# A scratch tile of the weight conversion in PSUM, three banks for the first products, and memsets on GpSimd, in a gated attention and expert kernel

## The chip, the core and the metric

The kernel runs on one core of a Trainium2 chip. The metric is the device time of one execution in microseconds. TensorE multiplies matrices, VectorE and ScalarE work elementwise on SBUF and PSUM, GpSimd elementwise on SBUF, and SyncE (SP) issues nearly all DMAs. PSUM has eight banks of 512 fp32 values in each of 128 partitions.

## What is computed

Three stages follow each other (the reference, cut):

```python
for t in range(S):                                   # gated linear attention, S = 768, 32 heads of 48
    state = f[t][..., None] * state + outer(k[t], v[t])
    y[t] = q[t] @ state
x = y as (3072, 384)
e_idx = argmax(x @ w_gate)                           # one of 8 experts for each token
for e in range(8):
    h = maximum(x[e_idx == e] @ w1[e], 0)            # 384 -> 1024
    x[e_idx == e] = gate * eom * (h @ w2[e])         # 1024 -> 384
h = x @ w_in                                         # 384 -> 2048
out = (h * cos(h)) @ w_out                           # 2048 -> 384
```

All is fp32. The kernel gets fp32 precision from TensorE by splitting every operand into a rounded part (`hi`, `wh`, `yh`) and the rest (`lo`, `wl`, `yl`) and adding three products.

## The kernel before, in words

The attention stage ends near 182 us. It scatters its tokens into a DRAM table `xs` that is sorted by expert. Then comes the stage of the experts, in `moe_ffn`, until near 450 us, and after it the last feed-forward network (FFN).

The experts' stage has NS = 64 steps, 8 for each of 8 experts. A loop at the end of the stage runs, for each step s:

- `mm1(s)` (the first product): nine matmuls of 448 columns (L628, L629, L631, in the helper `first_product`) into a bank of the pool `ps_h`. ScalarE writes `hi` = relu (L190) and VectorE `lo` (L191); both read the bank, `lo` last. The pool has four banks.
- `mm2(s - 2)` (the second product): nine matmuls (L202 to L204) from `hi` and `lo` of step s - 2 into three banks `o`, which hold the expert's sum over its 8 steps. After an expert's last step VectorE and ScalarE copy the sums into `yT` (L212 to L215), at a place that is read from a register.
- the events listed for the step by `at(s, ...)`, called by one line, L326, in the order in which they were listed.

So the order on each engine's queue is written out by hand. The events are:

- Weights. A ring of split weights is filled some ten half blocks ahead. In each step a half block of 128 x 768 that lies in `ws` is split: ScalarE rounds two quarters (L114), GpSimd subtracts for the first, VectorE for the second (both L118). Then SP issues the next load into the `ws` buffer that comes free (L101), and waits for both subtractions before it.
- Tokens of the next expert. At step 8e + 7 SP writes a list of token numbers (L180) and issues four loads `xe` (L163). In steps 8e + 4 to 8e + 6 TensorE transposes 128 columns each (`trans_x`, L170) into the one bank of `ps_t`; ScalarE and VectorE split it (L620 and L621). The next transposition needs the bank empty.
- Conversion of the FFN's weights. They arrive in a 64-bit form, and 24 pieces of 128 x 512 are turned into fp32 and stored to DRAM. `conv_load` (L221) is three steps ahead of `conv_a`, and `conv_b` and `conv_store` (L246) follow a step after that; a piece starts every 2.3 steps from step 6 on. The two buffers of `cs` are freed by `conv_b`.
- In steps 0 to 5 twelve memsets clear `yT`, two in a step, after the step's split.

A conversion is one ScalarE instruction, Abs into the tile `a` (L228), and seven of VectorE: L229 writes the sign bits of `cs` into the tile `b`, L230 and L231 change `a` in place, L233 puts `a` and `b` together into `a`; then in `conv_b` L239 writes the exponents of `a` into `b`, L240 multiplies `b` with the low words of `cs`, L242 adds `b` to `a`. In the profile the tiles are called `ca` and `cb`. Both lie in SBUF; `cb` has one buffer.

PSUM is full in this stage: three banks `ps_o`, four `ps_h`, one `ps_t`.

Of the kernel before, what the change touches and what calls it, by code (L numbers as in the profile page):

```python
# [9 lines left out]
I32 = mybir.dt.int32  # L10
# [4 lines left out]
PSUM = bass.MemoryType.PSUM  # L15
# [32 lines left out]
def build(tc, A, O):  # L48
    nc = tc.nc
    sp = nc.sync  # L50
    with ExitStack() as top:
        const = top.enter_context(tc.tile_pool(name="const", bufs=1))
        dram = top.enter_context(tc.tile_pool(name="dram", bufs=1, space=DRAM))
        xs = dram.tile([XROWS, XW], F32, name="xs")
        idtab = dram.tile([NT + CAP, 1], I32, name="idtab")
        wffn = dram.tile([8, 128, PW], F32, name="wffn")

        ident = const.tile([128, 128], F32, name="ident")
        ones = const.tile([128, 128], BF16, name="ones")
        zeros = const.tile([128, 128], BF16, name="zeros")  # L60
        ctab = const.tile([128, E, GMAX], F32, name="ctab")
        acc = const.tile([128, E], BF16, name="acc")
        plast = const.tile([128, NU, NP], F32, name="plast")
        flag = const.tile([128, 1], I32, name="flag")

        with tc.manual_schedule(), ExitStack() as rows:
            c = dict(locals())
            c["W"] = W = Weights(tc, A, c, top)
            c["ya"] = top.enter_context(tc.tile_pool(name="ya", bufs=1, side="right"))
            c["xa"] = rows.enter_context(tc.tile_pool(name="xa", bufs=1, side="right"))  # L70
            attention(tc, A, c)
            W.more(top)
            moe_ffn(tc, A, O, c)
        general(tc, A, O, c)
# [50 lines left out]
def moe_ffn(tc, A, O, c):  # L125
    nc = tc.nc
    pe, dve, act, pool, sp = nc.tensor, nc.vector, nc.scalar, nc.gpsimd, nc.sync
# [4 lines left out]
    HP = PW // 3  # L132
    LAG1 = 2
    with ExitStack() as ctx:
        keep = ctx.enter_context(tc.tile_pool(name="keep", bufs=1))
        yT = keep.tile([128, KD, NT + CAP], F32, name="yT")
        start = keep.tile([128, E], I32, name="start")
        flag = c["flag"]
        reuse = dict(reuse_waits="tile")
# [10 lines left out]
        with ExitStack() as mctx:  # L150
            xb = mctx.enter_context(tc.tile_pool(name="xb", bufs=1, **reuse))
            cv = mctx.enter_context(tc.tile_pool(name="cv", bufs=1, **reuse))
            hp = mctx.enter_context(tc.tile_pool(name="hp", bufs=LAG1 + 1, **reuse))
            ps_o = mctx.enter_context(tc.tile_pool(name="ps_o", bufs=1, space=PSUM, **reuse))
            ps_h = mctx.enter_context(tc.tile_pool(name="ps_h", bufs=4, space=PSUM, **reuse))
            ps_t = mctx.enter_context(tc.tile_pool(name="ps_t", bufs=1, space=PSUM, **reuse))

            xe, xT, hh, yps = {}, {0: c["xT0"]}, {}, {}
# [65 lines left out]
            def conv_a(i):  # L224
                v = cvt[i].bitcast(I32).rearrange("p (n two) -> p n two", two=2)
                a = cv.tile([128, HP], F32, name="ca", bufs=2)
                b = cv.tile([128, HP], I32, name="cb")
                act.activation(out=a, in_=v[:, :, 1].bitcast(F32), func=AF.Abs)  # L228
                dve.tensor_scalar(out=b, in0=v[:, :, 1], scalar1=-2 ** 31, scalar2=None, op0=ALU.bitwise_and)  # L229
                dve.tensor_scalar(out=a, in0=a, scalar1=F64_LO, scalar2=F64_HI, op0=ALU.max, op1=ALU.min)  # L230
                dve.tensor_scalar(out=a.bitcast(I32), in0=a.bitcast(I32), scalar1=0x08000000, scalar2=3,  # L231
                                  op0=ALU.bitwise_xor, op1=ALU.logical_shift_left)
                dve.scalar_tensor_tensor(out=a.bitcast(I32), in0=a.bitcast(I32), scalar=0x7FFFFFFF, in1=b,  # L233
                                         op0=ALU.bitwise_and, op1=ALU.bitwise_or)
                cvt[i] = (v[:, :, 0], a, b)
# [43 lines left out]
            def at(s, fn, *a):  # L279
                ev.setdefault(s, []).append((fn, a))  # L280
# [7 lines left out]
            for i in range(24):  # L288
                t = 6 + 23 * i // 10
                at(t - 3, conv_load, i)  # L290
                at(t, conv_a, i)
                at(t + 1, conv_b, i)
                at(t + 1, conv_store, i)
# [13 lines left out]
            at(3, ids, 0)  # L307
            q = (NT + CAP) // 4
            for i in range(12):
                at(i // 2, dve.memset, yT[:, i // 4, i % 4 * q:(i % 4 + 1) * q], 0.0)  # L310
            for e in range(E - 1):
                for d in range(KD):
                    at(8 * e + 4 + d, trans_x, e + 1, d)
# [20 lines left out]
        with ExitStack() as fctx:  # L334
# [4 lines left out]
            ps_h = fctx.enter_context(tc.tile_pool(name="ps_h2", bufs=4, space=PSUM, **reuse))  # L339
# [871 lines left out]
```

## Time and profile before

| what | us |
| --- | --- |
| three runs | 848.99, 855.98, 854.69 |
| median | 854.69 |
| the profiled execution | 861.5 |
| its span | 859.3 |

The profiled execution's time is its span and 2.2 us around it. Over the span TensorE is busy for 823.4 us (96%), VectorE for 667.9 (78%), ScalarE for 380.6 (44%), GpSimd for 357.4 (42%). A busy TensorE says little by itself: its records overlap, and they are longer when the granted clock is lower, so the idle time and the clock are read together. [...] In a row of the timeline, what stands in brackets is the engine's idle time before the instruction and what ended it. In a row by line, three durations are the shortest, the median and the longest; a duration holds the time in which the instruction was held up on its engine.

### The profile page before, as it was taken

The numbers are of one execution on the slowest core, as the hardware profiler recorded it, in microseconds if no ns is written. First come the engines' busy times: TensorE is split into PE (matmuls) and PEld (weight loads), VectorE is DVE, ScalarE is ACT, GpSimd is POOL, SyncE is SP. The second block draws the span as 40 slices with busy tenths as digits, with TensorE's granted clock in tenths as the row PEclk, the third lists the DMA queues.
The fourth block names the chain that finished last, engine by engine and source line by source line (L and its number), as shares of the span: only waits on it lengthen the run. The fifth ranks groups of instructions, "written<-read, shape, count | busy, mean of one in ns | idle before, by whom it ended". The sixth has DMA issues, their size and how long they took to land.

```text
span 859.3 us, 14492 instructions
## 1 busy us (share of the span) xinstructions
PE 823.4 (96%) x5316; PEld 736.0 (86%) x5316; DVE 667.9 (78%) x1213; ACT 380.6 (44%) x737; POOL 357.4 (42%) x331
## 2 busy tenths in 40 slices
PE   7998999999889988989999999999999999999996
PEld 6886888878788988979998999999999999998886
DVE  5576787779778898789969887777787687788990
ACT  5574776464434434344544443333333333333440
POOL 5014443332213222232246665455455554455752
PEclk9998999999989999999999999999999999999999
DMA  8996775238787877769751000000000000000001
GB/s 197 342 314 173 201 190 151 75 112 176 175 160 245 180 186 232 133 211 218 182 137 38 2 0 28 10 1 19 19 1 19 19 1 11 28 1 9 29 1 42
DMA packets 45298, 91.69 MB, mean 107 GB/s; under 512 B 12864, under 2 KB 23232, under 8 KB 45216
## 3 DMA queue, kind: packets, MB, share of 16 engines
q1 hardware_dynamic: 42144, 81.20, 36.1%
q0 software_dynamic: 3072, 9.45, 3.0%
q8 instruction: 44, 0.72, 0.4%
q14 instruction: 38, 0.31, 0.1%
HBM read 69.34 MB, written 21.29 MB: 105 GB/s over the span
## 4 chain that ended last, share of the span: by engine, by line
PE 71%; DVE 12%; DMA 10%; issue 4%; ACT 2%; POOL 1%; SPq 0%; POOLq 0%; DVEq 0%; ACTq 0%
PE ps L628 9%; PE ps L629 9%; PE ps L631 9%; PE o L380 7%; PE o L378 7%; PE o L379 7%; DMA cs<-in_wffn 4%; PE xps L839 3%; PE sps L752 3%; PE o L202 2%; DMA ws<-in_wmoe 2%; PE o L203 2%; PE o L204 2%; PE yps L791 2%; PE yps L801 2%
## 5 line engine op out<-in xcount | busy, mean ns | idle before, releaser
L374 POOL TENSOR_TENSOR lo<-r,hi 128x512 fp32r<-128x512 f32 (+1 forms) x96 | 149.3, 1555 | 171.0 <-ACT hi L373 91.5
L118 POOL TENSOR_TENSOR wl<-ws,wh 128x384 fp32r<-128x384 f32 x96 | 102.7, 1070 | 220.2 <-ACT wh L114 173.1
L628 PE MATMUL ps<-yh,wh 128*128 128x512 f32 (+1 forms) x480 | 187.2, 390 | 0.3 <-ACT yh L620 0.3
L629 PE MATMUL ps<-yh,wl 128*128 128x512 f32 (+1 forms) x480 | 185.4, 386 | 0.0
L631 PE MATMUL ps<-yl,wh 128*128 128x512 f32 (+1 forms) x480 | 132.8, 385 | 0.0
L373 ACT CAST hi<-r 128x512 fp32r<-128x512 f32 (+1 forms) x96 | 56.2, 586 | 168.5 <-DVE r L368 166.6
L380 PE MATMUL o<-wh,lo 128*128 128x384 f32 x352 | 119.2, 339 | 0.9 <-POOL lo L374 0.5
L636 DVE TENSOR_SCALAR n<-ps 128x512 f32<-128x512 f32 x96 | 66.2, 690 | 68.6 <-PE ps L631 68.6
L378 PE MATMUL o<-wl,hi 128*128 128x384 f32 x352 | 118.6, 337 | 0.0
L379 PE MATMUL o<-wh,hi 128*128 128x384 f32 x352 | 118.4, 336 | 0.0
L631 PEld LDWEIGHTS ps<-yl,wh 128*128 128x128 f32 x480 | 91.3, 190 | 15.8
L644 ACT ACTIVATE r<-r,quarter 128x512 f32<-128x512 f32 x96 | 69.5, 724 | 73.5 <-DVE r L643 73.5
L628 PEld LDWEIGHTS ps<-yh,wh 128*128 128x128 f32 x480 | 91.5, 191 | 11.7 <-ACT yh L620 0.4
L629 PEld LDWEIGHTS ps<-yh,wl 128*128 128x128 f32 x480 | 91.4, 190 | 11.0
L114 ACT CAST wh<-ws 128x384 fp32r<-128x384 f32 x160 | 75.0, 510 | 0.4 <-DMA ws<-in_wmoe 0.4
L643 DVE SCALAR_TENSOR_TENSOR r<-n,r 128x512 f32<-128x512 f32 x96 | 69.5, 724 | 3.3
L190 ACT ACTIVATE hi<-ps 128x448 fp32r<-128x448 f32 x64 | 34.9, 545 | 82.8 <-PE ps L631 82.8
L204 PE MATMUL o<-lo,wh 128*128 128x448 f32 x192 | 70.4, 367 | 0.7 <-DVE lo L191 0.7
L202 PE MATMUL o<-hi,wh 128*128 128x448 f32 x192 | 70.9, 369 | 0.0
L203 PE MATMUL o<-hi,wl 128*128 128x448 f32 x192 | 70.7, 368 | 0.0
L379 PEld LDWEIGHTS o<-wh,hi 128*128 128x128 f32 x352 | 66.1, 188 | 4.3
L378 PEld LDWEIGHTS o<-wl,hi 128*128 128x128 f32 x352 | 66.2, 188 | 3.9
(159 smaller groups left out, 1451.2 us busy)
## 6 DMA issues: line engine op xcount, KB each, us to landing
ws<-in_wmoe SPq DMA_DIRECT2D x64, 384.0 KB
cs<-in_wffn SPq DMA_DIRECT2D x24, 512.0 KB
kq<-in_qkf SPq DMA_DIRECT2D x46, 192.0 KB
wffn<-ca SPq DMA_DIRECT2D x24, 256.0 KB
ws<-wffn SPq DMA_DIRECT2D x16, 384.0 KB
xs<-xe SPq DMA_DIRECT2D x7, 770.0 KB
v<-in_v SPq DMA_DIRECT2D x24, 200.0 KB
xe<-xs SPq DMA_DIRECT2D x28, 168.4 KB
```

Source lines behind the costliest of these rows:

```text
L114: self.nc.scalar.copy(out=h, in_=w)
L118: (eng or self.nc.gpsimd).tensor_tensor(out=l, in0=w, in1=h.bitcast(F32), op=ALU.subtract)
L202: pe.matmul(yps[e][d], wh[:, cs], hi, start=m == 0, stop=False)
L203: pe.matmul(yps[e][d], wl[:, cs], hi, start=False, stop=False)
L204: pe.matmul(yps[e][d], wh[:, cs], lo, start=False, stop=m == FT - 1)
L374: pool.tensor_tensor(out=los, in0=r[:, cs], in1=his.bitcast(F32), op=ALU.subtract)
L378: pe.matmul(o, hi, wl[:, cs], start=m == 0, stop=False)
L379: pe.matmul(o, hi, wh[:, cs], start=False, stop=False)
L380: pe.matmul(o, lo, wh[:, cs], start=False, stop=m == NF - 1)
L628: nc.tensor.matmul(out, wh[:, ws[d]], xh[:, d, :], start=d == 0, stop=False)
L629: nc.tensor.matmul(out, wl[:, ws[d]], xh[:, d, :], start=False, stop=False)
L631: nc.tensor.matmul(out, wh[:, ws[d]], xl[:, d, :], start=False, stop=d == 2)
```

## The change

The tile `b` of the conversion comes from a new PSUM pool of one bank, in place of SBUF. The pool of the first products has three banks in place of four. The twelve memsets of `yT` go from VectorE's queue to GpSimd's, at the same places in the order.

```diff
-            ps_h = mctx.enter_context(tc.tile_pool(name="ps_h", bufs=4, space=PSUM, **reuse))
+            ps_h = mctx.enter_context(tc.tile_pool(name="ps_h", bufs=3, space=PSUM, **reuse))
+            ps_c = mctx.enter_context(tc.tile_pool(name="ps_v", bufs=1, space=PSUM, **reuse))
...
                 a = cv.tile([128, HP], F32, name="ca", bufs=2)
-                b = cv.tile([128, HP], I32, name="cb")
+                b = ps_c.tile([128, HP], I32, name="cb")
...
             for i in range(12):
-                at(i // 2, dve.memset, yT[:, i // 4, i % 4 * q:(i % 4 + 1) * q], 0.0)
+                at(i // 2, pool.memset, yT[:, i // 4, i % 4 * q:(i % 4 + 1) * q], 0.0)
```

## Rows read from the trace of the kernel before

**Rows 1.** Stretches: stretch, length, busy PE, PEld, DVE, ACT, POOL, PEclk, DMA, GB/s

```profile
182.00:450.00 268.00, 251.92 (x1243) 229.78 (x1243) 227.75 (x357) 121.05 (x260) 78.72 (x77) 0.97 0.74 185
...
262.00:282.00 20.00, 18.42 (x98) 16.82 (x97) 18.25 (x29) 9.51 (x20) 6.15 (x6) 1.00 0.60 192
...
302.00:322.00 20.00, 17.78 (x85) 16.15 (x84) 18.49 (x33) 8.16 (x17) 4.95 (x5) 0.91 0.81 200
```

**Rows 2.** Waits of TensorE, 182 to 450 us: total us, times, longest

```profile
PE ps L170 <- DVE yl L621: 15.1, 6, 5.3
PE o L204 <- DVE lo L191: 0.7, 1, 0.7
PE ps L628 <- ACT yh L620: 0.3, 1, 0.3
```

**Rows 3.** TensorE's timeline, the six waits of a transposition: start, us

```profile
202.39 0.60 PE L170 MATMUL ps<-ident,xe 112*128 112x112 f32 x4 [0.91 <-DVE yl L621]
...
238.53 1.01 PE L170 MATMUL ps<-ident,xe 112*128 112x112 f32 x4 [5.33 <-DVE yl L621]
...
273.33 0.60 PE L170 MATMUL ps<-ident,xe 112*128 112x112 f32 x4 [1.58 <-DVE yl L621]
...
306.18 1.01 PE L170 MATMUL ps<-ident,xe 112*128 112x112 f32 x4 [2.22 <-DVE yl L621]
...
340.39 1.01 PE L170 MATMUL ps<-ident,xe 112*128 112x112 f32 x4 [2.28 <-DVE yl L621]
...
376.18 0.60 PE L170 MATMUL ps<-ident,xe 112*128 112x112 f32 x4 [2.79 <-DVE yl L621]
```

**Rows 4.** VectorE's timeline, from the run ahead of the second wait

```profile
226.43 0.43 DVE L229 TENSOR_SCALAR cb<-cs 128x512 int32<-128x512 int32 x1 [3.85 <-DMA cs<-in_wffn]
...
228.91 1.47 DVE L233 SCALAR_TENSOR_TENSOR ca<-ca,cb 128x512 int32<-128x512 int32 x1
...
233.18 1.43 DVE L242 TENSOR_TENSOR ca<-ca,cb 128x512 f32<-128x512 f32 x1
...
237.86 0.62 DVE L621 TENSOR_TENSOR yl<-ps,yh 128x448 fp32r<-128x448 f32 x1
```

**Rows 5.** By line, tile `cb`: shortest, median, longest ns

```profile
L229 DVE TENSOR_SCALAR cb<-cs x24: 408/418/428, 206.1 to 427.7; 128x512 int32<-128x512 int32 x24
...
L239 DVE TENSOR_SCALAR cb<-ca x24: 409/418/1198, 210.2 to 432.5; 128x512 int32<-128x512 int32 x24
...
L240 DVE SCALAR_TENSOR_TENSOR cb<-cs,cb x24: 691/693/1395, 211.2 to 433.0; 128x512 f32<-128x512 uint32 x24
```

**Rows 6.** Memsets by line (shortest, median, longest ns); one row of GpSimd's timeline

```profile
L326 DVE MEMSET yT<- x12: 792/792/792, 187.4 to 204.4; 128x880 f32 x12
...
L1012 POOL MEMSET xe<- x1: 1390/1390/1390, 10.4 to 10.4; 128x1540 f32 x1
...
193.01 1.01 POOL L118 TENSOR_TENSOR wl<-ws,wh 128x384 fp32r<-128x384 f32 x1 [2.64 <-ACT wh L114]
```

**Rows 7.** By line, VectorE in the FFN: shortest, median, longest ns

```profile
L636 DVE TENSOR_SCALAR n<-ps x96: 677/691/692, 451.5 to 833.2; 128x512 f32<-128x512 f32 x96
...
L368 DVE TENSOR_TENSOR r<-r,ps x96: 672/679/686, 455.1 to 837.6; 128x512 f32<-128x512 f32 x96
...
L637 DVE TENSOR_SCALAR n<-n x96: 426/427/1220, 452.2 to 833.9; 128x512 f32<-128x512 f32 x96
```

**Rows 8.** Groups of VectorE, 182 to 450 us: busy us, mean ns, idle before

```profile
L242 DVE TENSOR_TENSOR ca<-ca,cb 128x512 f32<-128x512 f32 x24 | 22.2, 925 | 0.8
...
L233 DVE SCALAR_TENSOR_TENSOR ca<-ca,cb 128x512 int32<-128x512 int32 x24 | 22.1, 919 | 0.8
...
L239 DVE TENSOR_SCALAR cb<-ca 128x512 int32<-128x512 int32 x24 | 17.3, 719 | 0.0
```

**Rows 9.** SP: a row of its waits, and one of its timeline

```profile
SPq L101 <- DVE wl L118: 116.0, 37, 13.3
...
213.34 0.35 SPq L221 DMA_DIRECT2D cs<-in_wffn  x1
```

## The prediction

> **What bounds the kernel now.** I read the stage table first, since the change touches the experts' stage alone. Between 182 and 450 us TensorE is busy for 251.9 of 268 us at a mean granted clock of 0.97 [rows 1]. The reader is to see two losses: 16.1 us of idle TensorE, and clock worth about 268 x 0.03 = 8.0 us. Without both the stage would take 244 us, so nothing done here can bring more than 24.1 us. Outside the stage the change touches nothing.
>
> Then the waits of TensorE [rows 2]: 15.1 us, in six waits, go to one pair: a transposition of the next expert's tokens (L170) waits until VectorE has emptied the only transposition bank (L621); 0.7 us more is one wait for `lo`. The timeline gives the six by size: 0.91, 5.33, 1.58, 2.22, 2.28 and 2.79 us [rows 3]. I call them A to F. Of the four larger ones the clock is the second price: the 20 us around D were granted 0.91, so 1.8 us more is lost there, those around C were granted 1.00 [rows 1]; an idle of 1.58 us cost no clock and one of 2.22 us did.
>
> Why L621 is late is in VectorE's timeline [rows 4]. Ahead of A VectorE is behind with memsets. Ahead of B it waits 3.85 us for a load of `cs` and then works back to back from 226.43 until L621 at 237.86, 11.4 us, while TensorE stands from 233.2 to 238.5 [rows 3]. In that run the two-input conversion steps L233 and L242 take 1.47 and 1.43 us, where such a step takes 0.69 undisturbed (L240's median) [rows 5]: GpSimd's split (L118) runs beside it. So the stage waits for a VectorE that is itself stretched by GpSimd. C to F have such a run ahead of them too.
>
> **The change part by part.**
>
> *Memsets.* Twelve of 0.792 us leave VectorE, 9.5 us, two in each of the steps 0 to 5 [rows 6]. A disappears: -0.9 us. On GpSimd a row of 1540 elements took 1.39 us [rows 6]; 880 elements are 0.79 by size alone, and I take 0.85, with 1.39 as the far end. Two in each step, 1.7 us, stand behind the step's split, in front of the next one's; from step 3 on GpSimd has 2.64 us idle there [rows 6], which hides even 2 x 1.39 but for 0.1 us. In steps 0 to 2 the splits come closer and two of them are pushed back by 1 to 2 us; who waits is SP's next `ws` load (L101), which today waits for VectorE's half of the split, itself behind the memsets. I take nothing for it. If that cover were gone, it is 2 us of load time once. The copies into yT (L212 to L215) now wait for GpSimd as well, but only after an expert's eighth step, when the memsets are over.
>
> *Three banks.* Nothing, and neither loss nor gain: before the first product of step s TensorE has already run the second product of step s-3, which needed that step's `lo`, and `lo` is the last reader of the bank that step s takes back. The wait is met by program order. The trace has no wait of a first product for its bank [rows 2].
>
> *The second tile in PSUM.* Five of the seven VectorE instructions of a conversion name it. Three (L233, L240, L242) had two inputs in SBUF and get one from PSUM. VectorE instructions with one input of each kind exist in the next stage: L368 stays between 672 and 686 ns in all 96 cases, while the SBUF-only L637 beside it is stretched from 426 to as much as 1220 [rows 7]. So the stretch should go: L233 from a mean of 919 to about 690, L242 from 925 to about 690 [rows 8]. The other two (L229, L239) lose: both run at 409 to 418 ns undisturbed from SBUF to SBUF [rows 5]; the only single-input row that touches PSUM, L636, takes 691 [rows 7]. No row shows VectorE writing to PSUM, so the price lies between 418 (no loss) and, far off, 1.395 us, the longest L240 [rows 5]. I take 690, the nearest row, for the three that write it. Over 24 conversions: +6.5 us (L229), 24 x (690 - 719) = -0.7 us (L239, whose mean is stretched today too), -5.5 us (L233), -5.6 us (L242) [rows 8]: -5.3 us of VectorE time in all, little for an engine that is busy 228 of 268 us. The 2-input and SBUF-only steps that remain (L118, L230, L231) are still open to GpSimd.
>
> What counts is the run ahead of each wait. Counted in the timeline there are ten stretched instructions of the freed kinds: L233, L240, L242 in B's run, two L233 in C's, one L233 in D's, L233 and L242 in each of E's and F's; each is some 0.75 us too long [rows 4]. Against them stand six L239 at +0.28 us (two ahead of C, one ahead of each of the others), and two L229 at +0.27 us, one each ahead of B and C; the other L229 start with a late load, and their extra is covered by ScalarE's Abs, for which L230 waits anyway. So:
> A 0.91 -> 0; B 5.33 - 2.25 + 0.55 = 3.6; C 1.58 - 1.5 + 0.83 = 0.9; D 2.22 - 0.75 + 0.28 = 1.75; E 2.28 - 1.5 + 0.28 = 1.05; F 2.79 - 1.5 + 0.28 = 1.55. The 0.7 us ahead of F (a wait for `lo`, behind L233) goes too.
> Idle falls from 15.8 to 8.85, by 7.0 us. D to F come down to the size of C, which cost no clock: three times 1.8 = 5.4 us of the 8.0 come back; 0 if the clock falls all the same. Sum: -12.4 us, or -7.0 if no clock comes back.
>
> [...]
>
> The profiled execution took 861.5 us, the runs' median is 854.69. If the difference is stage idle too, the runs lose 17.3 us where the profile loses 24.1, and the gain scales to 8.9 us: 845.8. Unscaled it is 842.3. I take **845.0 us**.
>
> **The rivals.**
> *Every wait goes (about 838 us).* SP waits 116 us for VectorE's splits before `ws` loads [rows 9], and the `cs` loads and the conversions' stores queue behind those; a VectorE that is earlier brings its own next load earlier. If that feeds on itself, all 24.1 us come back: 861.5 - 24.1 = 837.4. Against: B is set by a load that SP issued at 213.34 and that landed at 226.4 [rows 4, 9].
> *Loads set it (about 853 us).* B begins with VectorE idle for `cs` [rows 4]; D and F do as well. If the transfers, not the issue, are late, a faster VectorE waits longer and only A and a part of the runs go: 1 to 3 us. Against: after the landing VectorE works back to back, and its length is what TensorE waits for.
> *The conflict moves (about 860 us).* GpSimd's splits, one in each step, still need about 1 us each [rows 6] with the shared access. If they now meet L118, L230 and L231 instead, the ten stretches stay and the full-rate price comes on top: B +0.55, C +0.83, D to F +0.28 each, less A, +1.3 us; C comes to 2.4 us and loses 1.8 us of clock as D does; the stores and loads that come later for it repeat some 2 us: about +5. It decides once more than about half of the 7.5 us is paid elsewhere. A PSUM write of over 1.2 us would do the same: the runs hold fourteen uncovered ones (two L229, six L239, six L240), and 14 x 0.5 us eats the 7.0.
> *Not doing what it says*: if the PSUM input did not free VectorE from GpSimd, L233 and L242 would keep means over 0.9 us; that comes to the former case.
>
> **How the numbers follow.** Forecast (840 to 850) 0.45, every wait goes 0.13, loads set it 0.27, the conflict moves 0.15. Over 1%, about what a measurement of this kernel can tell from no change, means below 846.1 or above 863.2. Three quarters of the forecast's chance and all of the first rival lie below: 0.47. Of the last rival a half lies above: 0.07. The rest, 0.46, is within. The range reaches from 837 (all idle gone) to 859 (most of the moved conflict).
>
> **What would show it.** Right: L233, L240 and L242 within 20 ns of 680 to 695; L229 and L239 near 690; yT's memsets near 0.85 us on GpSimd; the wait at 202 us gone; L170's waits for L621 at some 9 us, and a clock of 0.98 or better in the stage. Wrong: L118 on VectorE well above its present mean, L621's waits at 15 us or more, a first product waiting for VectorE or ScalarE at its bank, or as much idle before L229 as saved elsewhere.

## The result, and the profile after

| what | before | after |
| --- | --- | --- |
| runs | 6 | 6 |
| median, us | 854.25 | 847.51 |
| lowest and highest, us | 848.99 and 856.55 | 843.90 and 849.42 |
| profiled execution, us | 861.5 | 847.61 |
| its experts' stage, us | 266.7 | 255.2 |

The ratio is 0.990, with a 95% interval of 0.9872 to 0.9928: 6 to 11 us faster. The profiled executions lie 13.9 us apart. Of that 11.6 us are the experts' stage, counted from its first product to the FFN's first product, and 2.7 us are the attention stage, which was just shorter in the second execution (the stage began at 179.82 in place of 182.50) and which the change doesn't touch. The profiled execution of the kernel before is also 5 us longer than the longest of its six runs. Such shifts between executions are why the medians and ratios decide below and the profiles only explain.

From the pools of PSUM on, lines of the kernel after are one higher than before: L229 to L242 of a conversion are L230 to L243, L170 is L171, L621 is L622, L326 is L327.

The whole stage first, from its own first product on; columns as in [rows 1]. Before, in a span of 859.3 us:

```profile
182.50:449.22 266.72, 250.95 (x1238) 229.04 (x1239) 227.33 (x355) 120.28 (x258) 78.43 (x75) 0.97 0.74 186
```

After:

```profile
179.82:434.97 255.15, 246.51 (x1237) 225.66 (x1238) 209.36 (x343) 120.67 (x258) 83.47 (x87) 0.99 0.77 194
```

Between these two executions TensorE's idle time falls from 15.8 to 8.6 us and its clock rises from 0.97 to 0.99. VectorE is busy 18.0 us less, GpSimd 5.0 us more. The waits of TensorE in the stage, which answer to [rows 2]:

```profile
PE ps L171 <- DVE yl L622: 8.6, 4, 4.1
PE ps L629 <- ACT yh L621: 0.3, 1, 0.3
```

In its timeline, the four that answer to the six of [rows 3]:

```profile
233.49 0.60 PE L171 MATMUL ps<-ident,xe 112*128 112x112 f32 x4 [4.14 <-DVE yl L622]
...
327.12 0.60 PE L171 MATMUL ps<-ident,xe 112*128 112x112 f32 x4 [0.33 <-DVE yl L622]
...
360.57 1.01 PE L171 MATMUL ps<-ident,xe 112*128 112x112 f32 x4 [2.81 <-DVE yl L622]
...
393.98 0.60 PE L171 MATMUL ps<-ident,xe 112*128 112x112 f32 x4 [1.36 <-DVE yl L622]
```

The first wait of before, near 202 us, is gone; the largest is 4.14 in place of 5.33. The steps that name `cb`, by line (shortest, median, longest ns), answer to [rows 5]:

```profile
L230 DVE TENSOR_SCALAR cb<-cs x24: 679/684/697, 202.1 to 414.0; 128x512 int32<-128x512 int32 x24
L234 DVE SCALAR_TENSOR_TENSOR ca<-ca,cb x24: 686/689/690, 204.3 to 416.5; 128x512 int32<-128x512 int32 x24
L240 DVE TENSOR_SCALAR cb<-ca x24: 676/683/685, 206.5 to 418.3; 128x512 int32<-128x512 int32 x24
L241 DVE SCALAR_TENSOR_TENSOR cb<-cs,cb x24: 695/696/697, 207.2 to 419.0; 128x512 f32<-128x512 uint32 x24
L243 DVE TENSOR_TENSOR ca<-ca,cb x24: 686/686/687, 207.9 to 419.7; 128x512 f32<-128x512 f32 x24
```

No step is stretched any more: the longest of the 120 takes 697 ns, where the longest of before took over 1.4 us. The two single-input steps went from 418 to 684 ns. The largest run of before [rows 4] has its counterpart in VectorE's timeline:

```profile
222.90 0.69 DVE L230 TENSOR_SCALAR cb<-cs 128x512 int32<-128x512 int32 x1 [4.56 <-DMA cs<-in_wffn]
...
225.38 0.69 DVE L234 SCALAR_TENSOR_TENSOR ca<-ca,cb 128x512 int32<-128x512 int32 x1
...
228.63 0.69 DVE L243 TENSOR_TENSOR ca<-ca,cb 128x512 f32<-128x512 f32 x1
...
232.82 0.62 DVE L622 TENSOR_TENSOR yl<-ps,yh 128x448 fp32r<-128x448 f32 x1
```

From the landing of `cs` to the split that TensorE waits for it takes 9.9 us in place of 11.4, but the landing itself is hardly earlier: it comes 43.1 us after the stage's first product in place of 43.9, and VectorE waits 4.56 us for it in place of 3.85.

### The profile page after: what moved, and what is told of

It reads as the page before. It is cut to its first block, busy times and chain, and to the rows that moved or that the text cites. A ratio compares the mean times of both kernels' runs of the same rounds, so it can differ in the third digit from the quotient of the medians.

```text
span 845.8 us, 14495 instructions
## 1 busy us (share of the span) xinstructions
PE 816.7 (97%) x5316; PEld 730.5 (86%) x5316; DVE 648.7 (77%) x1201; ACT 380.9 (45%) x737; POOL 363.4 (43%) x343
## 4 chain that ended last, share of the span: by engine, by line
PE 72%; DMA 11%; DVE 11%; issue 3%; ACT 1%; POOL 1%; SPq 0%; POOLq 0%; DVEq 0%; ACTq 0%
PE ps L629 10%; PE ps L630 10%; PE ps L632 10%; PE o L381 7%; PE o L379 7%; PE o L380 7%; DMA cs<-in_wffn 4%; PE o L203 3%; PE o L204 3%; PE o L205 3%; DMA f<-in_ft 3%; DMA kq<-in_qkf 2%; PE xps L840 2%; PE sps L753 2%; PE yps L792 2%
## 5 line engine op out<-in xcount | busy, mean ns | idle before, releaser
L375 POOL TENSOR_TENSOR lo<-r,hi 128x512 fp32r<-128x512 f32 (+1 forms) x96 | 147.1, 1533 | 171.6 <-ACT hi L374 91.0
L118 POOL TENSOR_TENSOR wl<-ws,wh 128x384 fp32r<-128x384 f32 x96 | 99.0, 1032 | 199.3 <-ACT wh L114 144.3
L629 PEld LDWEIGHTS ps<-yh,wh 128*128 128x128 f32 x480 | 90.8, 189 | 11.6 <-ACT yh L621 0.4
```

What stands on the lines that cost most here:

```text
L118: (eng or self.nc.gpsimd).tensor_tensor(out=l, in0=w, in1=h.bitcast(F32), op=ALU.subtract)
L375: pool.tensor_tensor(out=los, in0=r[:, cs], in1=his.bitcast(F32), op=ALU.subtract)
L629: nc.tensor.matmul(out, wh[:, ws[d]], xh[:, d, :], start=d == 0, stop=False)
```

## The experiments

Each kernel is held against runs of the kernel before on the same chip; the level of those differs by some us from one set of runs to another, so ratios are compared.

**e1_memsets and e2_psum: the two parts alone.** The first is the kernel before with this:

```diff
-                at(i // 2, dve.memset, yT[:, i // 4, i % 4 * q:(i % 4 + 1) * q], 0.0)
+                at(i // 2, pool.memset, yT[:, i // 4, i % 4 * q:(i % 4 + 1) * q], 0.0)
```

The second is the kernel after with that line as it was.

> The kernel before with only the twelve memsets moved to GpSimd; the conversion's second tile stays in SBUF and the first products keep four banks. Theory (the parts add up, the PSUM tile carries the gain): only the wait near 200 us goes, 0.9 us, and SP's early weight loads come some 2 us sooner, so about 853 us against 854, a ratio of 0.998. Rival (the early start carries the gain, because each earlier load brings the next one sooner): 849 us or less, a ratio of 0.994 or below, with the later waits of the transpositions clearly under 15 us.

> The kernel after with the memsets back on VectorE; the second tile in PSUM and three banks. Theory: most of the gain, 5 to 6 us, so 848 to 849 us, a ratio of 0.993 to 0.994; the wait near 200 us is back at about 0.9 us; L233, L240 and L242 of the first trace stay near 0.69 us with hardly any spread. Rival (the early start carries the gain): 852 us or more, a ratio above 0.997.

Measured: 0.9992 (0.9960 to 1.0023) for the memsets, 0.9937 (0.9901 to 0.9972) for the PSUM tile. In the profiles the transpositions waited 13.4 us in five places with the memsets moved, without the one near 200 us, and 8.8 us in five with the tile moved, the first of them at 201.53 with 1.81 us. So the memsets' part is the early wait and can't be told from nothing in the time, and the kernel with the tile carries the gain. Within their intervals the two add up to the whole. The early wait was 1.81 us with the tile moved, twice what it had been before; and e2_psum holds the three banks too, which the next pair takes by themselves.

**e3_banks3 and e5_three_kept: the three banks alone.** The edit of both, in the kernel before:

```diff
-            ps_h = mctx.enter_context(tc.tile_pool(name="ps_h", bufs=4, space=PSUM, **reuse))
+            ps_h = mctx.enter_context(tc.tile_pool(name="ps_h", bufs=3, space=PSUM, **reuse))
```

> The kernel before with three banks for the first products and nothing else; one bank stays empty. Theory (program order meets the wait): no difference, a ratio of 0.998 to 1.002, and no wait of a first product for VectorE's lo in the trace. Rival (the bank count matters where VectorE is late): 1 to 4 us slower, with waits of L628 for L191.

It came out at 1.0037 (1.0004 to 1.0070), a little slower, and not as the theory or the rival has it: no first product waits for a bank in its trace. TensorE's timeline shows another wait, at the very start of the stage:

```profile
182.62 0.17 PE L255 MATMUL ps<-acc,ones 128*128 128x8 bf16 x1 [2.04 <-DVE yl L621]
```

L255 counts the tokens of each expert and is the first user of the transposition bank. With seven banks in use that bank had moved one place down, onto one that, as the wait says, L621 still had to read for attention's tokens. In the two kernels compared here L255 doesn't wait. So e5_three_kept adds a tile that holds the empty bank, as the change itself does:

```diff
+            ps_c = mctx.enter_context(tc.tile_pool(name="ps_v", bufs=1, space=PSUM, **reuse))
             ps_t = mctx.enter_context(tc.tile_pool(name="ps_t", bufs=1, space=PSUM, **reuse))
...
             def guards():
+                dve.memset(ps_c.tile([128, HP], F32, name="none")[:, 0:1], 0.0)
```

> Three banks for the first products in the kernel before, as in e3_banks3, but the bank that comes free is held by a tile that only one small memset writes, so that the transposition bank stays where it was. Theory (what e3_banks3 lost came from the transposition bank moving one place down, onto the bank that attention's last split still reads, with the wait of the count's matmul at L255): no wait before that matmul, and a ratio of 0.998 to 1.002. Rival (three banks themselves cost): 1.003 or more again, with a lower granted clock or later lo somewhere in the steps.

Measured: 0.9981 (0.9948 to 1.0013), with no wait before that matmul. Three banks cost nothing that these runs can tell. Against e2_psum (0.9937) the intervals still meet, so these two alone don't separate the tile from the bank that it holds. The whole change does: memsets and banks without the tile come by estimate to 0.9992 x 0.9981 = 0.997, with some 0.0045 either way, and the change gave 0.990 twice.

The profiled execution of e5_three_kept is also a warning. Its conversion steps are stretched as before (its L234 and L243, L233 and L242 of before, took up to 1495 and 1399 ns), and yet its stage and its transpositions' waits are near those of the kernel after:

```profile
181.42:438.58 257.16, 248.33 (x1238) 226.56 (x1239) 226.07 (x356) 121.16 (x258) 77.19 (x75) 0.98 0.75 192
```

```profile
PE ps L171 <- DVE yl L623: 8.7, 5, 3.1
```

VectorE waited 6.2 us for `cs` in it, where it waited 12.0 in the profile of before. So a fall of these waits from 15 to 9 us between two profiles is by itself no proof of the change; its ratio and the shorter run behind a landing are.

**e10_writes: what stretched the steps.** GpSimd keeps its place and writes, but reads nothing:

```diff
-        (eng or self.nc.gpsimd).tensor_tensor(out=l, in0=w, in1=h.bitcast(F32), op=ALU.subtract)
+        if eng is self.nc.gpsimd:
+            eng.memset(l.bitcast(F32), 0.0)
+            eng.memset(l.bitcast(F32), 0.0)
+        else:
+            (eng or self.nc.gpsimd).tensor_tensor(out=l, in0=w, in1=h.bitcast(F32), op=ALU.subtract)
```

> The kernel before, but GpSimd's half of each split in the experts' stage is left out and two memsets of the same quarter stand in its place, so GpSimd is busy for a similar time and writes the same place but reads nothing; the low parts of half of the weights are zero in that stage. Theory (a step with two SBUF inputs meets GpSimd's reads only, a step at double rate meets any GpSimd work): L233, L240, L242 and VectorE's L118 lose their spread, maximum below 0.75 us, while L231 and L239 keep some stretched cases above 0.6 us. Rival one (any GpSimd work stretches all of them): maxima above 1 us in all. Rival two (only GpSimd's reads stretch anything): none is stretched.

By line, with lines four higher than before for the conversion (L233 is L229 of before, L237 is L233, and so on; L122 is VectorE's half of the split, L118 of before):

```profile
L233 DVE TENSOR_SCALAR cb<-cs x24: 415/418/762, 202.1 to 400.7; 128x512 int32<-128x512 int32 x24
L237 DVE SCALAR_TENSOR_TENSOR ca<-ca,cb x24: 691/693/695, 203.4 to 402.3; 128x512 int32<-128x512 int32 x24
L243 DVE TENSOR_SCALAR cb<-ca x24: 414/417/691, 206.2 to 403.9; 128x512 int32<-128x512 int32 x24
L244 DVE SCALAR_TENSOR_TENSOR cb<-cs,cb x24: 691/693/694, 206.6 to 404.4; 128x512 f32<-128x512 uint32 x24
L246 DVE TENSOR_TENSOR ca<-ca,cb x24: 691/692/695, 207.3 to 405.1; 128x512 f32<-128x512 f32 x24
...
L122 DVE TENSOR_TENSOR wl<-ws,wh x64: 546/551/561, 183.5 to 418.7; 128x384 fp32r<-128x384 f32 x64
```

All steps with two SBUF inputs have lost their spread, while those at double rate, as the expectation calls it (L233, L243: one input, medians of 418 and 417 ns where the steps with two inputs take 692 and 693), are still stretched at times, to 762 and 691. That is the first theory as these rows show it: with a GpSimd that reads, in the kernel before, L233 and L118 took up to 1496 and 1404 ns, with one that only writes they took at most 695 and 561, while steps at double rate were stretched with both (L239 of before to 1198 ns). The timelines rule out that the two engines just no longer met. Of the 136 executions of L233, L240, L242 and L118 in the kernel before, 32 were more than a fifth too long, each with a GpSimd instruction beside it; of the 136 of L237, L244, L246 and L122 here, 35 had a memset of GpSimd beside them, and none was stretched. In the kernel after 53 of the 120 executions of the five steps that name `cb` had a split of GpSimd beside them, and none was stretched.

The stage of this kernel, from its first product to the FFN's, has a clock of 1.00 and 0.3 us of idle TensorE; counted like this the prediction's floor is 266.7 - 15.8 - 8.0 = 242.9:

```profile
179.78:422.55 242.77, 242.51 (x1238) 223.33 (x1238) 187.63 (x355) 121.07 (x258) 61.12 (x140) 1.00 0.80 204
```

The ratio, from two runs, is 0.9787 (0.9736 to 0.9838), though VectorE still waits 8.1 us for `cs` in it. One reservation: GpSimd is also busy for less time (61 against 78 us), since two memsets of a quarter take 0.88 us, and its half of the split no longer waits for ScalarE or holds a `ws` buffer. So the rows show what stretched the steps; how much of the time this alone is worth, the ratio doesn't show.

**e8_first_half and e9_second_half: where the tile in PSUM pays.** One half of the conversion keeps its second tile in SBUF, `cd`:

```diff
             def conv_b(i):
                 low, a, b = cvt.pop(i)
+                b = cv.tile([128, HP], I32, name="cd")
```

is e8; in e9 `conv_a` has the `cv.tile` and `conv_b` the `ps_c.tile`. After_again is the kernel after, beside them.

> The kernel after once more, on the chip of the runs beside it, so that they can be held against it. Theory: the same ratio as before, 0.988 to 0.993, and a stage of the experts of 253 to 258 us with 7 to 11 us of waits of the transpositions. Rival (the first profile was a lucky one): a stage above 260 us.

> The kernel after, but the second half of a conversion (L239, L240, L242 of the first trace) gets a tile of its own in SBUF; only L229 and L233 have theirs in PSUM. Theory (each stretch that is freed pays, each double rate that is lost costs): by the counts of the prediction the first half frees six stretches of 0.75 us against two uncovered L229 of 0.27, so most of the gain stays: a ratio of 0.991 to 0.995, L233 at 0.69 us without spread, L242 stretched again to a mean above 0.85. Rival (the conflict is only moved): L242 and L118 take what L233 was freed of, and the ratio is 0.996 or more.

> The kernel after, but the first half of a conversion (L229, L233 of the first trace) gets a tile of its own in SBUF; only L239, L240 and L242 have theirs in PSUM. Theory: four freed stretches (3.0 us) against six L239 of 0.28 us (1.7 us), so a small gain from this half: a ratio of 0.994 to 0.998, with L233 at a mean above 0.85 us. Rival (what counts is when conv_b ends, because SP's store and the next load wait for it): as good as the whole change, 0.992 or below.

Measured: 0.9902 (0.9868 to 0.9936) for the kernel after, with a stage of 258.8 us, just longer than expected, and 9.5 us of waits; 0.9952 (0.9922 to 0.9982) for the first half alone; 0.9932 (0.9905 to 0.9958) for the second. In VectorE's groups of e8 (busy us, mean ns) the conflict shows where it is still possible:

```profile
L118 DVE TENSOR_TENSOR wl<-ws,wh 128x384 fp32r<-128x384 f32 x61 | 48.0, 786 | 1.7 <-ACT wh L114 1.7
...
L244 DVE TENSOR_TENSOR ca<-ca,cd 128x512 f32<-128x512 f32 x24 | 20.9, 870 | 0.8
```

(L244 is L242 of before), and of e9, where L232 and L234 are L231 and L233 of before:

```profile
L232 DVE TENSOR_SCALAR ca<-ca 128x512 int32<-128x512 int32 x24 | 25.6, 1066 | 0.8
L234 DVE SCALAR_TENSOR_TENSOR ca<-ca,cd 128x512 int32<-128x512 int32 x24 | 23.8, 992 | 0.8
```

With the first half freed, L118 on VectorE rises from its 714 ns of before to 786: part of the conflict is moved, as the rival says. With the second half freed L118 falls to 648 (63 splits), though the first half is stretched a little more than before (L234 at 992 against 919 ns). Each half alone gives a part; which is worth more the intervals don't tell, and my count, by which the first half should be the larger, found no support: the first half came out just short of its expected range, the second just better than its own.

**e4_list_act, e6_cs3, e11_both_psum, e12_both: what is left.** After the change TensorE still waits 8.6 us, all but the 0.33 behind late loads of `cs`. Where these loads lose their time is seen in the stretches of the kernel after (columns as in [rows 1]) behind a token list's write, which SP issued at 206.48:

```profile
210.00:212.00 2.00, 2.00 (x12) 1.71 (x11) 1.97 (x4) 0.59 (x2) 1.02 (x1) 1.00 0.56 23
212.00:214.00 2.00, 2.00 (x11) 1.83 (x11) 1.77 (x5) 0.84 (x2) 0.00 (x0) 1.00 1.19 32
214.00:216.00 2.00, 2.00 (x12) 1.82 (x11) 1.60 (x4) 0.91 (x4) 0.00 (x0) 1.00 0.47 29
216.00:218.00 2.00, 2.00 (x12) 1.81 (x11) 1.97 (x4) 0.94 (x3) 1.02 (x1) 1.00 0.51 59
218.00:220.00 2.00, 2.00 (x11) 1.84 (x10) 0.34 (x1) 0.00 (x0) 0.00 (x0) 1.00 1.07 361
```

For 8 us 23 to 59 GB/s move, and only then 361; a `cs` load issued at 209.32 lands at 222.9. Most packets that start in these 8 us (187 of 209) are of 1540 bytes, rows of the `xe` loads that SP issues behind the write. That the slow stretch comes with the write and not with them, two other places in this trace show: behind the write issued at 401.85, the last, SP issues no `xe` load, and 40 GB/s moved from 405.9 to 411.9; the first `xe` loads have no such write ahead of them, and 249 GB/s moved from 185.2 to 189.2.

e4 issues that write from ScalarE's queue, the rest as in the kernel after:

```diff
-                s = nc.values_load(start[0:1, e:e + 1], engines=[mybir.EngineType.SP], min_val=0, max_val=NT,
+                s = nc.values_load(start[0:1, e:e + 1], engines=[mybir.EngineType.Activation], min_val=0, max_val=NT,
...
-                sp.dma_start(out=idtab[bass.ds(s, CAP), :].rearrange("(r p) one -> p r one", p=RT), in_=t.bitcast(I32))
+                act.dma_start(out=idtab[bass.ds(s, CAP), :].rearrange("(r p) one -> p r one", p=RT), in_=t.bitcast(I32))
```

> The kernel after with the write of the token list into idtab issued from ScalarE's queue in place of SP's. Theory for what is left (8.6 us of idle TensorE in four waits): the loads of the conversion are late because they queue behind that write of 4-byte elements, which holds SP's transfers for 8 to 9 us once per expert; off that queue the loads land sooner, the waits of the transpositions fall to 3 us or less and the time to 840 to 844 us. Rival one (the write takes the same 16 DMA engines wherever it is issued, and ScalarE loses issue time in front of hi): 847 to 849 us with the waits unchanged. Rival two (what is left is VectorE's own length after the landing): the waits for cs shrink, but the transpositions still wait 6 us or more.

Measured: 0.9864 (0.9811 to 0.9917). VectorE's waits for `cs` fall from 14.8 to 7.6 us, but the transpositions wait 6.6 us. That is the second rival by its number, but not in full by its reason, for one of the four waits is the edit's own:

```profile
200.18 0.55 ACT L191 ACTIVATE hi<-ps 128x448 fp32r<-128x448 f32 x1 [7.11 <-DMA id<-xs]
```

```profile
203.20 0.60 PE L171 MATMUL ps<-ident,xe 112*128 112x112 f32 x4 [2.05 <-DVE yl L622]
```

ScalarE, which now has the first list's write in its queue, stands 7.11 us until that list has been loaded; `hi` and VectorE's `lo` and split come late behind it, and TensorE waits 2.05 us at a place where the kernel after has no wait. This is what rival one feared of ScalarE. The other three waits come to 4.5 us. The interval doesn't tell the kernel from the kernel after.

e6 leaves the queue as it is and asks for the loads earlier:

```diff
-                t = cv.tile([128, HP], mybir.dt.int64, name="cs", bufs=2)
+                t = cv.tile([128, HP], mybir.dt.int64, name="cs", bufs=3)
...
-                at(t - 3, conv_load, i)
+                at(t - 5, conv_load, i)
```

> The kernel after with three buffers for the conversion's input and its load issued five steps ahead in place of three. Theory (what is left begins with a load that comes late, 14.8 us of VectorE's waiting for cs in five places): the waits for cs fall below 5 us, the transpositions' waits below 4 us, and the ratio is 0.980 to 0.986. Rival (SP issues in order, and the loads are late because SP and the transfers are, so the earlier place only pushes other loads back): waits for cs above 10 us and a ratio of 0.988 to 0.993.

Measured: 0.9824 (0.9791 to 0.9857), 839.79 us beside 855.87 of the kernel before. VectorE waits for `cs` no more; the transpositions' waits and the stage:

```profile
PE ps L171 <- DVE yl L622: 2.0, 4, 1.4
```

```profile
179.82:425.25 245.43, 243.38 (x1237) 223.02 (x1238) 206.78 (x343) 120.94 (x258) 84.26 (x87) 1.00 0.79 202
```

This is the theory: the late loads are what the change left. The stage is within 2.7 us of the 242.8 of e10_writes. It is the version that beats both kernels, with an interval below that of the kernel after. The same two numbers in the kernel before, without the tile in PSUM, were not run, so how much of this gain needs the tile is open. VectorE's remaining conflict is still there (L231 of this kernel has a mean of 813 ns), at hardly a price, because VectorE now has the time.

e11 uses the one bank for both halves, so that every step but the first has an operand in PSUM, and none two inputs from SBUF (the six have means of 681 to 699 ns in its profile):

```diff
-                b = ps_c.tile([128, HP], I32, name="cb")
-                act.activation(out=a, in_=v[:, :, 1].bitcast(F32), func=AF.Abs)
+                b = cv.tile([128, HP], I32, name="cd")
+                p = ps_c.tile([128, HP], F32, name="cb", tag="cb")
+                act.activation(out=p, in_=v[:, :, 1].bitcast(F32), func=AF.Abs)
...
             def conv_b(i):
+                b = ps_c.tile([128, HP], I32, name="cb", tag="cb")
```

with L230, L231 and L233 of before working on `p`. e12 is e11 and e4 together.

> A version that goes further with the same bank: ScalarE's Abs writes into PSUM, L230 and L231 of the first trace work there in place, L233 takes that tile and the sign bits from SBUF, and conv_b uses the bank for its own second tile. All VectorE steps of a conversion but the first then have at most one SBUF input and no double rate. Theory (the stretch of the remaining SBUF steps, means of 0.74 us against 0.43, is worth more than their double rate): seven steps take 0.42 + 6 x 0.69 = 4.56 us against 4.92, VectorE's run after a late load is shorter by up to 0.6 us where GpSimd's splits fall into it, and the ratio is 0.985 to 0.990. Rival (the bank is now shared by both halves, so ScalarE's Abs waits for conv_b and holds up hi behind it): slower than the kernel after, a ratio above 0.993, with waits of ScalarE for VectorE at Abs.

> Two steps beyond the kernel after together: e11_both_psum and the token list's write from ScalarE's queue as in e4_list_act. Theory (they act on the two halves of a late run, the landing and the work after it): a ratio of 0.978 to 0.985, with waits for cs of about 8 us and the transpositions' waits below 6 us. Rival (each only gives what the other would have given, or ScalarE's new waits eat it): 0.986 or more.

e11 gave 0.9872 (0.9834 to 0.9911), within the interval of the kernel after beside it (0.9902), so it decides nothing; ScalarE's Abs waits 6.8 us for `conv_b`, as the rival feared. In its profile, the longest of its five runs, the transpositions wait 12.6 us. e12 gave 0.9843 (0.9809 to 0.9877), the theory's upper end, with 7.7 us of waits for `cs` and 4.7 us of the transpositions', of which 1.6 is the early wait of e4 again. The intervals of both meet that of e6, which does it by two numbers.

## Why the prediction was right

The forecast was 845.0 us in a range of 837 to 859; it became 847.5. Measured against its own base, the median of 854.69, it promised 9.7 us; the ratio of 0.990 is 8.5 us of 854. The mechanism was right for the steps and for the run ahead of the largest wait; the count wait by wait was not, and its sum was luck.

- *The price of PSUM.* Taken at 690 ns for a step that writes PSUM, measured 684 for L230, 683 for L240, 696 for L241. The nearest row (L636, 691 ns with a PSUM input of f32) was right for an output too, and for steps of int32 (L230, L240), which no row of before could show. A PSUM input in place of one from SBUF made neither of these two-input steps slower: L234 and L243, with one PSUM input, take 689 and 686 ns where L233 and L242 took 693 and 692 undisturbed before.
- *The stretch goes.* L233 and L242 of before came from means of 919 and 925 to 688 and 686, with no spread. e10_writes shows the cause. The run ahead of B became 1.5 us shorter (11.4 to 9.9), where three freed steps less the two that slow down were counted at 2.25 - 0.55 = 1.7. That is the mechanism of the prediction, measured at the place where it was to act.
- *The memsets.* 0.85 us was taken, 0.832 measured. The early wait went. SP's waits for GpSimd ahead of `ws` loads are 2.2 us in place of 1.8, next to nothing as taken. Alone the memsets are not measurable (e1_memsets).
- *Three banks.* No wait of a first product for its bank; e5_three_kept confirms it. Only the place of the other banks mattered, as e3_banks3 showed by accident (2.04 us ahead of L255), and the prediction did not consider that. The change keeps it by putting its new pool in the gap.
- *The waits.* The sum came out at 8.6 us where 8.85 was worked out, and the clock at 0.99. That is luck. Each wait belongs to the second transposition of its expert, so they can be matched: A went; B is 4.14 in place of 3.6; C and D are gone, where 0.9 and 1.75 were left; E is 0.33 in place of 1.05; F is 2.81 in place of 1.55, no shorter than before; and the 1.36 us at 393.98 is a seventh wait, one expert further, which the prediction did not have. The clock went the same way: by 20 us stretches from the stage's first product only those of B and F were granted 0.91, the others 1.00, while F was one of the three whose clock was to come back. In after_again the same kernel has waits of 4.55, 1.81, 0.34 and 2.79 us at B, D, E and F, and e5_three_kept came to 8.7 us with nothing freed. By e5_three_kept and e6_cs3, what is left of each wait hangs on how late the loads land in that execution, and the count took the landings as fixed.
- *The conflict moves.* It hardly did. The groups of the kernel after:

```profile
L118 DVE TENSOR_TENSOR wl<-ws,wh 128x384 fp32r<-128x384 f32 x64 | 43.3, 676 | 2.2 <-ACT wh L114 2.2
...
L232 DVE TENSOR_SCALAR ca<-ca 128x512 int32<-128x512 int32 x24 | 17.8, 742 | 0.8
L231 DVE TENSOR_SCALAR ca<-ca 128x512 f32<-128x512 f32 x24 | 17.7, 736 | 1.2 <-ACT ca L229 1.1
```

Before, these three had means of 714, 1031 and 457 ns. L231 and L232 share 35.5 us where they had 35.7. The stretch moved one step ahead within the pair: 11 of 24 L231 and 9 of 24 L232 took over 0.6 us, where 1 and 19 had; that L230 takes longer is a likely reason, not a shown one. VectorE's half of the split is a little shorter. In e8_first_half, where the second half stays in SBUF, the split does take a part over (786 ns).

- *Loads set it.* I gave this 0.27 as the whole story. It is the story of the rest: e6_cs3 took the remaining idle time out, but for 2.0 us, by touching nothing but the loads. VectorE's waits for `cs` grew from 12.0 to 14.8 us, which looks like the prediction's sign "as much idle before L229 as saved elsewhere". But they were 13.8 and 16.3 in e2_psum and after_again, and 13.5, 14.9 and 6.2 in e1_memsets, e3_banks3 and e5_three_kept, whose tile lies in SBUF. So 2.8 us is within what executions differ by, and that freed time became waiting is not shown.
- *The scaling to the median.* The stage's 11.6 us in the profiles met the 12.4 of the sum. In the medians it is 6.7 us, or 8.5 by the ratio, near the scaled 8.9. That the timed runs of the kernel before lose less in this stage than its profiled execution was an assumption. It was not tested by itself; the other profiles with the tile in SBUF have stages of 262.7 (e1_memsets), 267.0 (e3_banks3) and 257.2 us (e5_three_kept) against its 266.7, so it was one of the long ones.

## What to carry to other kernels

Where VectorE and GpSimd worked side by side here, an operand of VectorE in PSUM took a two-input step out of the conflict at no cost (L233 and L242 of before: means of 919 and 925 ns, then 688 and 686), while a step that ran at double rate from SBUF to SBUF paid 0.27 us for 512 columns (418 to 684 ns). Both counts come from the rows, but they are worth something only in the run that another engine waits for. Before shortening such a run, ask why it starts late: here two numbers that bring a load forward (e6_cs3), on top of the change, gave three quarters as much again. Before a change is credited with a wait that shrank between two profiles, look at another profile without it: here one such kernel had waits as short (e5_three_kept). And the pool of banks that shrank in e3_banks3 moved its neighbour, by the wait of 2.04 us at L255; look at who last used the place that a bank moves to.

## What the runs showed of the hardware that was not expected

- Whether a memset on GpSimd disturbed VectorE depended in e10_writes on the step beside it: all 136 executions of L237, L244, L246 and L122 stayed undisturbed (longest 695 ns, and 561 for L122), 35 of them with a memset beside them, while a double-rate step was stretched from 415 to 762 ns.
- Behind a write of 448 elements of 4 bytes (issued at 206.48) SP's transfers in the kernel after moved at 23 to 59 GB/s for 8 us. With the write issued from ScalarE they were as slow: from 216 to 222 us in e4_list_act 48 to 71 GB/s moved.
- In e3_banks3 the idle of 2.04 us ahead of L255 was followed by first products that start 0.37 us apart in place of 0.20, and the stretch from 184 to 202 us was granted 0.91, where the kernel before had 1.00: 18 x 0.09 = 1.6 us more, so in this execution the wait was paid almost twice.
